# One product moved from VectorE to GpSimd, and the picks paired, in a top-k attention followed by a capacity-limited mixture of experts

## The chip, the core and the metric

The kernel runs on one NeuronCore of one Trainium2 chip. A core has five engines that run their own instruction queues in order and meet at semaphores: TensorE (PE: matrix products and transposes), VectorE (DVE), ScalarE (ACT), GpSimd (POOL), and SyncE (SP), which here only issues transfers. The metric is the device time of one execution in microseconds (us); lower is better. Before the change it is 997.43 us, the median of three runs (995.88 to 999.83).

## The reference

Attention over 8 batches of 8 heads, 576 tokens, head width 64, in which each row of scores keeps only its 32 largest entries; then a routing of the 4608 tokens to 8 experts, of which each takes the 80 tokens with the highest gate.

```python
def _attn_ref(q, k, v):                      # (8, 8, 576, 64)
    scores = scale * np.matmul(q, k.transpose(0, 1, 3, 2))
    kth = np.partition(scores, -32, axis=-1)[..., -32:-31]
    mask = scores >= kth
    scores = np.where(mask, scores, -1e9)
    attn = softmax(scores)                   # written out in the reference
    return np.matmul(attn, v)

def _moe_ref(x, w_gate, w1, w2, capacity):   # x (4608, 512), 8 experts, capacity 80
    logits = x @ w_gate
    expert_idx = np.argmax(logits, axis=1)
    gate_w = softmax(logits)[np.arange(N), expert_idx]
    for e in range(E):
        tok_idx = ...                        # the 80 tokens of expert e with the largest gate_w
        h = np.maximum(x[tok_idx] @ w1[e], 0.0)
        out[tok_idx] = gate_w[tok_idx, None] * (h @ w2[e])
```

## The kernel before

The attention part is a software pipeline. A *unit* is one tile of 128 query rows of one head, so a unit is a 128 x 576 tile of scores `s`; 32 pairs of heads have nine units each (four row tiles for each of two heads, and one last tile that holds the 64 remaining rows of both heads), 288 in all. They are numbered through, and a *step* `i` of the pipeline issues, for several units at once, the piece that each is due for. Steps come in pairs: an even one and an odd one.

For each unit the threshold is found so. Six maxima over sixths of the row give 48 candidates (`parts`); three rounds of "take the eight largest" over these give the 24th largest candidate (`search`). ScalarE then computes the sign of each score against that value and counts them; the scores times the signs are formed, the eight largest of that product are taken, and a *pick* by the count selects the threshold. `below` makes a mask of the scores that fall under it.

```python
def search(self, i):
    s, cand = self.s[i], self.top[i]
    ...
    for r in range(G0 // 8):                             # letters a, c, e: maxima
        dst = top[:, r, :] if r < G0 // 8 - 1 else w9[:, :8]
        nc.vector.max(out=dst, in_=cand)
        if r == G0 // 8 - 1:
            sign = self.rows.tile([P, S], BF16, name="sign", tag="sign")
            cnt = self.small.tile([P, 1], F32, name="cnt", tag="cnt")
            nc.scalar.activation(sign, s, Act.Sign, bias=w9[:, 7:8], scale=-1.0, accum_out=cnt)
        yield
        if r < G0 // 8 - 1:                              # letters b, d
            nc.vector.match_replace(out=cand, in_to_replace=dst, in_values=cand, imm_value=LOW)
            yield
    y = self.rows.tile([P, S], F32, name="y", tag="y", bufs=1)
    engine = nc.gpsimd if i in self.odd else nc.vector
    engine.tensor_tensor(out=y, in0=s, in1=sign, op=Alu.mult)   # letter y
    yield
    nc.vector.max(out=w9[:, 8:], in_=y)                  # letter g
    yield
    pick = ...
    nc.vector.scalar_tensor_tensor(out=pick, in0=past, scalar=cnt, in1=w9[:, 7:], accum_out=self.thr[:, i : i + 1],
                                   op0=Alu.is_equal, op1=Alu.mult)      # letter h
    yield

def below(self, i):                                      # letter m
    self.mask[i] = self.rows.tile([P, S], BF16, name="mask", tag="mask", bufs=3)
    if i in self.odd:
        nc.scalar.activation(self.mask[i], self.s[i], Act.Relu, bias=self.thr[:, i : i + 1], scale=-1.0)
        return
    nc.gpsimd.tensor_scalar(self.mask[i], self.s[i], self.thr[:, i : i + 1], None, op0=Alu.is_lt)
```

So before the change an even unit has its product on VectorE and its mask on GpSimd, an odd unit its product on GpSimd and its mask on ScalarE.

A step issues these pieces by a string of letters. `back` says how many steps after its own the unit gets the piece; `G` is one of the six maxima of the newest unit, and `z` a reciprocal of row sums.

```python
back = dict(a=0, b=1, c=1, d=1, e=1, y=2, g=3, h=4, m=4)
for c in "ghmGbGycGdGGGeaz" if i % 2 else "GbGhmgcGdGeGGyaz":
    ...
```

The remaining pieces of a step follow: `turn_w` (TensorE transposes the scores of a whole row tile and adds the masks, ScalarE takes the exponential), `front` (the scores of a later tile), `back` (the product with v, one step after `turn_w`), `divide`, and pieces of `norm`, which stores the result of a pair of heads and adds up its part of the gate's logits:

```python
def back(self, n, t):
    m = P if t < NF else TL                              # TL = 64 rows in the last tile
    for h in range(2):
        o = slice(2 * P + h * (D + 1), 2 * P + (h + 1) * (D + 1))
        j = h if t < NF else 0
        for c in range(NK):
            for r in range(0, m, TL):
                r0 = r if t < NF else TL * h
                nc.tensor.matmul(cc[r : r + TL, o], lhsT=wT[:, ..., r0 : r0 + TL], rhs=vb[:, c, h, :], ...)

# in norm
    nc.scalar.copy(part, lp[:, cs])
    yield 0
    if hp > 0:
        nc.vector.tensor_tensor(out=lg, in0=lg, in1=part, op=Alu.add)
```

Weights of experts 0 to 3 are loaded during the attention; expert 4 has a place of its own that comes free only when the attention's buffers do, and experts 5 to 7 follow into places that are done with. The part after the attention is routing (`route`) and eight experts (`finish`).

Of the kernel before, what the change touches and what calls it, by code (L numbers as in the profile page):

```python
# [9 lines left out]
F32 = mybir.dt.float32  # L10
# [4 lines left out]
Act = mybir.ActivationFunctionType  # L15
# [12 lines left out]
def kernel(  # L28
# [11 lines left out]
    nc = tc.nc  # L40
# [108 lines left out]
    class Attention:  # L149
# [95 lines left out]
        def search(self, i):  # L245

            s, cand = self.s[i], self.top[i]
            top = self.top[i] = self.small.tile([P, G0 // 8 - 1, 8], F32, name="top", tag="top")
            w9 = self.small.tile([P, 16], F32, name="w9", tag="w9")
            for r in range(G0 // 8):  # L250
# [8 lines that stand above are left out]
                if r < G0 // 8 - 1:  # L259
                    nc.vector.match_replace(out=cand, in_to_replace=dst, in_values=cand, imm_value=LOW)  # L260
                    yield
            y = self.rows.tile([P, S], F32, name="y", tag="y", bufs=1)
            engine = nc.gpsimd if i in self.odd else nc.vector
            engine.tensor_tensor(out=y, in0=s, in1=sign, op=Alu.mult)  # L264
            yield
            nc.vector.max(out=w9[:, 8:], in_=y)  # L266
            yield
            pick = self.small.tile([P, TOP_K - G0 + 1], F32, name="pick", tag="pick")
            nc.vector.scalar_tensor_tensor(out=pick, in0=past, scalar=cnt, in1=w9[:, 7:], accum_out=self.thr[:, i : i + 1],  # L269
                                           op0=Alu.is_equal, op1=Alu.mult)  # L270
            yield
# [10 lines left out]
        def search_all(self, i):  # L282

            s = self.s[i]
            top = self.top[i] = self.small.tile([P, TOP_K // 8, 8], F32, name="top", tag="top")
            scr = self.rows.tile([P, S], F32, name="y", tag="y", bufs=1)
            nc.vector.max(out=top[:, 0, :], in_=s)
            for r in range(1, TOP_K // 8):
                nc.vector.match_replace(out=scr, in_to_replace=top[:, r - 1, :], in_values=s if r == 1 else scr,
                                        imm_value=LOW)  # L290
                nc.vector.max(out=top[:, r, :], in_=scr)
            nc.vector.tensor_copy(self.thr[:, i : i + 1], top[:, TOP_K // 8 - 1, 7:8])
# [35 lines left out]
        def back(self, n, t):  # L328

            wT, cc = self.w.pop((n, t))  # L330
            vb = self.vb[n % len(self.vb)]
            m = P if t < NF else TL
            for h in range(2):
                o = slice(2 * P + h * (D + 1), 2 * P + (h + 1) * (D + 1))
                j = h if t < NF else 0
                for c in range(NK):
                    for r in range(0, m, TL):
                        r0 = r if t < NF else TL * h
                        nc.tensor.matmul(cc[r : r + TL, o], lhsT=wT[:, j * NF + c if c < NF else 2 * NF + j, r0 : r0 + TL],  # L339
                                         rhs=vb[:, c, h, :], start=(c == 0), stop=(c == NF))  # L340
            self.w[n, t] = cc

        def over(self, n, t):


            m = P if t < NF else TL
            sums = self.w[n, t][:m, 2 * P : 2 * P + 2 * (D + 1)].rearrange("p (h d) -> p h d", h=2)[:, :, D]
            z = self.z[:m, n % NP, t, :]
            if self.lean:
                nc.vector.tensor_scalar(z, sums, EPS, None, op0=Alu.add)  # L350
            nc.vector.reciprocal(z, z if self.lean else sums)  # L351

        def divide(self, n, t):
            m = P if t < NF else TL
            if t == 0:
                self.xn[n] = self.rows.tile([P, NK, 2, D], F32, name="xn", tag="xn")
            cc = self.w.pop((n, t))
            for h in range(2):
                o = 2 * P + h * (D + 1)
                nc.scalar.activation(self.xn[n][:m, t, h, :], cc[:m, o : o + D], Act.Copy, scale=self.z[:m, n % NP, t, h : h + 1])  # L360

        def norm(self, n, b, hp, bi, nb, cs=range(NK)):


            xn = self.xn[n].rearrange("p c h d -> p c (h d)")
            one, cols = bass.ds(b, 1), slice(hp * P, (hp + 1) * P)
            full = [c for c in cs if c < NF]
            if full:
                nc.sync.dma_start(xv[one, : NF * P, cols].rearrange("o (c p) d -> p (o c) d", p=P), xn[:, :NF, :])
            if NF in cs:  # L370
                nc.sync.dma_start(xv[one, NF * P :, cols].rearrange("o p d -> p o d"), xn[:TL, NF:, :])
            yield 1
            ps = self.four()[:, :2, :].rearrange("p j c -> p (j c)")
            at = slice(cs[0] * P, min(S, cs[-1] * P + P))
            self.turn_in(ps, xn, cs)
            xT = self.xT
            nc.scalar.copy(xT[:, at], ps[:, at])
            yield 1
            lp = self.four()[:, 0, : NK * E].rearrange("p (c e) -> p c e", e=E)
            for c in cs:  # L380
                for r in range(0, P, TL):
                    nc.tensor.matmul(lp[r : r + TL, c, :], lhsT=xT[:, c * P + r : c * P + r + TL], rhs=wg[:, hp, :],
                                     start=True, stop=True)
            if bi == 0 and hp == 0:
                self.lg = self.small.tile([P, nb, NK, E], F32, name="lg", tag="lg", bufs=2)
            cs = slice(cs[0], cs[-1] + 1)
            lg = self.lg[:, bi, cs]
            part = lg if hp == 0 else self.small.tile([P, NK, E], F32, name="part", tag="part", bufs=2)[:, cs]
            nc.scalar.copy(part, lp[:, cs])  # L389
            yield 0  # L390
            if hp > 0:
                nc.vector.tensor_tensor(out=lg, in0=lg, in1=part, op=Alu.add)
            if hp == HP - 1 and bi == nb - 1 and cs.stop == NK:
                yield 0
                yield from self.gates(b - bi, nb)
# [32 lines left out]
        def run(self, slow):  # L428
# [17 lines left out]
            def step(i, last):  # L446
# [7 lines left out]
                        due.append(n + 1)  # L454
                    first[i] = self.parts(i)

                back = dict(a=0, b=1, c=1, d=1, e=1, y=2, g=3, h=4, m=4)

                for c in "ghmGbGycGdGGGeaz" if i % 2 else "GbGhmgcGdGeGGyaz":
                    if c == "G":  # L460
                        if 0 <= i < NU:
                            next(first[i])
                    elif c == "a":
                        if 0 <= i < NU:
                            next(first[i], None)
                            second[i] = self.search(i)
                            next(second[i])
                    elif c == "z":
                        for u in drawn:
                            self.over(*u)  # L470
                    elif c == "m":
                        if 0 <= i - back[c] < NU:
                            self.below(i - back[c])
                    elif i - back[c] in second:
                        next(second[i - back[c]])
# [257 lines left out]
    def finish(wpool, full):  # L733

        stack = ctx.enter_context(ExitStack())
        late = stack.enter_context(tc.tile_pool(name="late", bufs=1))
        for dma in load_w(4, late):
            dma()
        sl = stack.enter_context(tc.tile_pool(name="sl", bufs=1))
        fs = stack.enter_context(tc.tile_pool(name="fs", bufs=2))  # L740
        ps_x = stack.enter_context(tc.tile_pool(name="ps_x", bufs=2, space=PSUM))
# [119 lines left out]

    slow = clear()
    with ExitStack() as main:
        wpool = main.enter_context(tc.tile_pool(name="wpool", bufs=4))
        for e in range(4):
            slow += load_w(e, wpool, 4)
        with ExitStack() as stack:
            att = Attention(stack, False)
            att.run(slow)
        finish(wpool, False)  # L870
    with tc.If(nc.values_load(bad[0:1, 0:1]) > 0):
# [4 lines left out]
            with tc.For_i(0, B) as b:  # L876
                att.batch(b)
        with ExitStack() as again:
            wpool = again.enter_context(tc.tile_pool(name="wpool2", bufs=4))
            for e in range(4):  # L880
                for dma in load_w(e, wpool):
                    dma()
            finish(wpool, True)
# [31 lines left out]
```

## Time and profile before

| | us |
|---|---|
| time, median of 3 runs | 997.43 |
| span of the profiled execution | 997.8 |
| of it up to the end of the attention's pipeline (last logits added) | about 870 |
| routing, to the first expert's gathered tokens | about 34 |
| eight experts and the stores | about 94 |

The share of busy time of an engine is an average over parts with different limits; the attention's pipeline is the longest part and the one that the change is about, so it is read by itself, in windows of 200 us. A line of a window gives start and end, length, then for each engine the time it was busy and the instructions in it, the clock that TensorE was granted, the share of the DMA engines and the rate. In groups of instructions, a line gives the source line, engine, operation, output and input with shapes and count, then the total and mean time, and last the idle time before such instructions with the one that ended it. In an excerpt of the timeline a line gives the start, the duration, and the instruction, and in brackets the idle time before it. On VectorE each instruction starts before the one ahead of it has fully drained, so what one adds to the queue is the distance from its start to the next start, and not its duration.

### The profile page before, as it was taken

To read this page: it belongs to the slowest core of one execution; us is meant where nothing else is said; L and a number is where in the kernel's file an instruction comes from. 1 tells how busy PE (TensorE), PEld (TensorE's weight loads), DVE (VectorE), ACT (ScalarE), POOL (GpSimd) and SP (SyncE) were. 2 spreads that over 40 slices of the span, in tenths; PEclk is the share of its full clock that TensorE was granted. 3 is DMA by queue.
4 is the path that set the end of the run, shared out by engine and by line. 5 is a ranking of instruction groups with operands and counts; after the bars stand their busy time and mean duration, and the time that the engine had idled before them with its cause. 6 is when DMAs were issued, how large, how long until landed. Compare 5 with 4: busy or idle time off the path is not lost.

```text
span 997.8 us, 35583 instructions
## 1 busy us (share of the span) xinstructions
PE 902.1 (90%) x13368; PEld 724.4 (73%) x13368; DVE 864.6 (87%) x5072; ACT 789.3 (79%) x1652; POOL 451.8 (45%) x330
## 2 busy tenths in 40 slices
PE   5899999999899999999899999998999998689996
PEld 3677777777777777777777777776777777578896
DVE  5999999999999999999999999999999999561110
ACT  3899999999889989999899999998899999501110
POOL 2455555545455455554454555554545455302111
PEclk9999999999999999999999999999999999978998
DMA  3445443333332323233332312222222200144920
GB/s 72 103 124 133 127 128 91 92 91 92 93 91 74 81 70 89 82 88 93 91 91 79 87 44 50 50 49 50 49 50 50 48 14 14 25 159 144 383 70 27
DMA packets 167893, 85.76 MB, mean 86 GB/s; under 512 B 117792, under 2 KB 154656, under 8 KB 167712
## 3 DMA queue, kind: packets, MB, share of 16 engines
q1 hardware_dynamic: 166688, 80.78, 29.3%
q0 software_dynamic: 1024, 2.62, 0.8%
q8 instruction: 107, 1.75, 0.7%
q14 instruction: 74, 0.61, 0.2%
HBM read 63.19 MB, written 20.19 MB: 84 GB/s over the span
## 4 chain that ended last, share of the span: by engine, by line
DVE 48%; PE 26%; ACT 19%; issue 6%; DMA 1%; POOL 0%; POOLq 0%; SPq 0%; ACTq 0%; DVEq 0%
DVE cand L241 15%; DVE w L266 11%; DVE cand L260 6%; DVE y L264 6%; PE cc L339 4%; PE sp L201 4%; ACT wT L325 4%; ACT sign L257 4%; PE yp L799 4%; ACT s L233 4%; DVE top L252 4%; ACT mask L278 3%; PE sp L226 3%; PE ab L316 3%; DVE pick L269 2%
## 5 line engine op out<-in xcount | busy, mean ns | idle before, releaser
L241 DVE MAX8 cand<-s 128x8 f32<-128x96 f32 x1728 | 388.6, 246 | 8.8 <-ACT s L233 8.8
L280 POOL TENSOR_SCALAR mask<-s,thr_all 128x576 bf16<-128x576 f32 x144 | 248.2, 1724 | 152.4 <-DVE pick L269 117.4
L264 POOL TENSOR_TENSOR y<-s,sign 128x576 f32<-128x576 f32 x144 | 184.7, 1283 | 271.9 <-DVE pick L269 125.7
L339 PEld LDWEIGHTS cc<-vb,wT 128*64 128x64 f32 x5760 | 199.3, 138 | 104.6 <-ACT wT L325 91.8
L339 PE MATMUL cc<-vb,wT 128*64 128x65 f32 x5760 | 221.6, 224 | 34.0 <-ACT wT L325 32.4
L257 ACT ACTIVATE sign<-s,w 128x576 bf16<-128x576 f32 x288 | 225.4, 783 | 24.3 <-DVE w L252 23.9
L266 DVE MAX8 w<-y 128x8 f32<-128x576 f32 x288 | 216.3, 751 | 2.5 <-POOL y L264 2.5
L226 PE MATMUL sp<-both 64*128 64x288 f32 (+1 forms) x1280 | 202.0, 435 | 15.0 <-ACT part L389 6.5
L233 ACT ACTIVATE s<-sp 128x1152 f32<-128x1152 f32 (+1 forms) x161 | 166.9, 1037 | 12.3 <-PE sp L226 12.3
L316 PE MATMUL ab<-ident,s 128*128 128x128 f32 x1148 | 174.9, 281 | 0.0
L325 ACT ACTIVATE wT<-ab 128x1024 f32<-128x1024 f32 (+1 forms) x159 | 148.9, 936 | 0.0
L226 PEld LDWEIGHTS sp<-both 64*128 64x128 f32 (+1 forms) x1280 | 105.5, 179 | 53.7 <-ACT part L389 8.5
L316 PEld LDWEIGHTS ab<-ident,s 128*128 128x128 f32 x1148 | 127.1, 141 | 11.6 <-issue 0.9
L321 PEld LDWEIGHTS <-mask 128*128 128x128 bf16 x1440 | 92.8, 98 | 34.8 <-POOL mask L280 18.9
L252 DVE MAX8 top<-cand 128x8 f32<-128x48 f32 x576 | 114.8, 199 | 0.0
L278 ACT ACTIVATE mask<-s,thr_all 128x576 bf16<-128x576 f32 x144 | 112.5, 781 | 0.0
L260 DVE MATCH_REPLACE8 cand<-top,cand 128x48 f32<-128x48 f32 x576 | 110.5, 192 | 0.1
L264 DVE TENSOR_TENSOR y<-s,sign 128x576 f32<-128x576 f32 x144 | 106.7, 741 | 1.3 <-ACT sign L257 0.8
L360 ACT ACTIVATE xn<-cc,z_all 128x64 f32<-128x64 f32 (+1 forms) x320 | 83.0, 318 | 1.3 <-DVE z_all L351 1.3
L316 PE MATMUL cc<-ident,s 128*128 128x128 f32 x288 | 78.7, 273 | 0.0
L323 ACT ACTIVATE wT<-cc 128x256 f32<-128x256 f32 (+1 forms) x160 | 56.6, 354 | 21.5 <-PE cc L321 20.8
L269 DVE SCALAR_TENSOR_TENSOR pick<-past,cnt,w 128x9 f32<-128x9 f32 x288 | 62.4, 217 | 0.0
(188 smaller groups left out, 964.0 us busy)
## 6 DMA issues: line engine op xcount, KB each, us to landing
w<-in_moe_w_dram SPq DMA_DIRECT2D x32, 512.0 KB, 4.3
w<-in_moe_w_dram SPq DMA_DIRECT2D x8, 2048.0 KB, 12.4
out_dram<-zero SPq DMA_DIRECT2D x9, 1024.0 KB, 6.5
qn<-in_q_dram SPq DMA_DIRECT2D x64, 128.0 KB, 2.5
kn<-in_k_dram SPq DMA_DIRECT2D x64, 128.0 KB, 2.4
vb<-in_v_dram SPq DMA_DIRECT2D x64, 128.0 KB, 2.4
xd<-xn SPq DMA_DIRECT2D x32, 256.0 KB, 4.1
qn<-in_q_dram SPq DMA_DIRECT2D x32, 32.0 KB, 2.3
```

The source lines that it names most:

```text
L226: nc.tensor.matmul(o, lhsT=qT[d, t * P : t * P + m], rhs=kT[d, j * HS : (j + 1) * HS], start=True, stop=True)
L233: nc.scalar.activation(s[:, j * HS : (j + w) * HS].rearrange("p (j c) -> p j c", c=HS), ps[:, j : j + w, :HS], Act.Copy, scale=TINY)
L241: nc.vector.max(out=cand[:, j, :], in_=s[:, j * S // NG : (j + 1) * S // NG])
L252: nc.vector.max(out=dst, in_=cand)
L257: nc.scalar.activation(sign, s, Act.Sign, bias=w9[:, 7:8], scale=-1.0, accum_out=cnt)
L260: nc.vector.match_replace(out=cand, in_to_replace=dst, in_values=cand, imm_value=LOW)
L264: engine.tensor_tensor(out=y, in0=s, in1=sign, op=Alu.mult)
L266: nc.vector.max(out=w9[:, 8:], in_=y)
L280: nc.gpsimd.tensor_scalar(self.mask[i], self.s[i], self.thr[:, i : i + 1], None, op0=Alu.is_lt)
L316: nc.tensor.matmul(dst[h][c], lhsT=sc[:, keys[c]], rhs=ident, start=c == 0 or (c == NF and h == 0), stop=False, is_transpose=True, skip_gr ...
L325: nc.scalar.activation(wT[:, : g * NF, :], ab.rearrange("p h c r -> p (h c) r")[:, : g * NF, :], Act.Exp, scale=scale / TINY)
L339: nc.tensor.matmul(cc[r : r + TL, o], lhsT=wT[:, j * NF + c if c < NF else 2 * NF + j, r0 : r0 + TL], rhs=vb[:, c, h, :], start=(c == 0), ...
```

## The change

All products by the sign now run on GpSimd, which takes VectorE's 144 of them away; `y` gets two buffers instead of one. The string of letters is rearranged: an odd unit's pick (`H`) and mask (`M`) come one step earlier in its life than before, right after the max over its product, so that both picks of a pair of steps stand side by side in the even step. In the even step the letters `m` (for the even unit whose pick is `h`) and then `y` (for the even unit two younger) both go to GpSimd, in that order; the max `g` over that `y` is the second letter of the odd step. For the last tile of a pair of heads the two heads' products with v go to the two halves of the output's partitions (and of the array's columns) rather than one after the other to the same half, so the reciprocal and the division read it there. The logits are added one step later. To pay for the buffers, the weights of expert 3 are no longer loaded during the attention but after it, ahead of those of expert 4.

```diff
-            y = self.rows.tile([P, S], F32, name="y", tag="y", bufs=1)
-            engine = nc.gpsimd if i in self.odd else nc.vector
-            engine.tensor_tensor(out=y, in0=s, in1=sign, op=Alu.mult)
+            y = self.rows.tile([P, S], F32, name="y", tag="y")
+            nc.gpsimd.tensor_tensor(out=y, in0=s, in1=sign, op=Alu.mult)
...
-            m = P if t < NF else TL
-            for h in range(2):
+            for h in range(2 if t < NF else 1):
                 o = slice(2 * P + h * (D + 1), 2 * P + (h + 1) * (D + 1))
-                j = h if t < NF else 0
                 for c in range(NK):
-                    for r in range(0, m, TL):
-                        r0 = r if t < NF else TL * h
-                        nc.tensor.matmul(cc[r : r + TL, o], lhsT=wT[:, j * NF + c if c < NF else 2 * NF + j, r0 : r0 + TL],
-                                         rhs=vb[:, c, h, :], start=(c == 0), stop=(c == NF))
+                    for r in range(0, P, TL):
+                        nc.tensor.matmul(cc[r : r + TL, o], lhsT=wT[:, h * NF + c if c < NF else 2 * NF + h, r : r + TL],
+                                         rhs=vb[:, c, h if t < NF else r // TL, :], start=(c == 0), stop=(c == NF))
...
             nc.scalar.copy(part, lp[:, cs])
             yield 0
+            yield 0
             if hp > 0:
                 nc.vector.tensor_tensor(out=lg, in0=lg, in1=part, op=Alu.add)
...
-                back = dict(a=0, b=1, c=1, d=1, e=1, y=2, g=3, h=4, m=4)
-
-                for c in "ghmGbGycGdGGGeaz" if i % 2 else "GbGhmgcGdGeGGyaz":
+
+                back = dict(a=0, b=1, c=1, d=1, e=1, y=2, g=3, h=4, m=4, H=3, M=3)
+                for c in "GgybGcGdGeGGza" if i % 2 else "GGghHmMybGcGdGeGza":
...
-        late = stack.enter_context(tc.tile_pool(name="late", bufs=1))
-        for dma in load_w(4, late):
-            dma()
+        late = stack.enter_context(tc.tile_pool(name="late", bufs=2))
+        for e in (3, 4):
+            for dma in load_w(e, late):
+                dma()
...
-        wpool = main.enter_context(tc.tile_pool(name="wpool", bufs=4))
-        for e in range(4):
+        wpool = main.enter_context(tc.tile_pool(name="wpool", bufs=3))
+        for e in range(3):
             slow += load_w(e, wpool, 4)
```

Left out of the diff: the same pool sizes in the fallback path, which does not run on these inputs, and the matching indices in `over` and `divide`.

More of the change, by code (lines that the diff above doesn't have):

```diff
@@ L285, in search_all @@
             top = self.top[i] = self.small.tile([P, TOP_K // 8, 8], F32, name="top", tag="top")
-            scr = self.rows.tile([P, S], F32, name="y", tag="y", bufs=1)
+            scr = self.rows.tile([P, S], F32, name="y", tag="y")
             nc.vector.max(out=top[:, 0, :], in_=s)
@@ L331, in back @@
             vb = self.vb[n % len(self.vb)]
-            m = P if t < NF else TL
-            for h in range(2):
+            for h in range(2 if t < NF else 1):
                 o = slice(2 * P + h * (D + 1), 2 * P + (h + 1) * (D + 1))
-                j = h if t < NF else 0
                 for c in range(NK):
-                    for r in range(0, m, TL):
-                        r0 = r if t < NF else TL * h
-                        nc.tensor.matmul(cc[r : r + TL, o], lhsT=wT[:, j * NF + c if c < NF else 2 * NF + j, r0 : r0 + TL],
-                                         rhs=vb[:, c, h, :], start=(c == 0), stop=(c == NF))
+                    for r in range(0, P, TL):
+                        nc.tensor.matmul(cc[r : r + TL, o], lhsT=wT[:, h * NF + c if c < NF else 2 * NF + h, r : r + TL],
+                                         rhs=vb[:, c, h if t < NF else r // TL, :], start=(c == 0), stop=(c == NF))
             self.w[n, t] = cc
         def over(self, n, t):
-            m = P if t < NF else TL
-            sums = self.w[n, t][:m, 2 * P : 2 * P + 2 * (D + 1)].rearrange("p (h d) -> p h d", h=2)[:, :, D]
-            z = self.z[:m, n % NP, t, :]
+            g = 2 if t < NF else 1
+            sums = self.w[n, t][:, 2 * P : 2 * P + 2 * (D + 1)].rearrange("p (h d) -> p h d", h=2)[:, :g, D]
+            z = self.z[:, n % NP, t, :g]
             if self.lean:
@@ L353, in divide @@
         def divide(self, n, t):
-            m = P if t < NF else TL
             if t == 0:
@@ L358, in divide @@
             for h in range(2):
-                o = 2 * P + h * (D + 1)
-                nc.scalar.activation(self.xn[n][:m, t, h, :], cc[:m, o : o + D], Act.Copy, scale=self.z[:m, n % NP, t, h : h + 1])
+                if t < NF:
+                    p, o, j, m = slice(0, P), 2 * P + h * (D + 1), h, P
+                else:
+                    p, o, j, m = slice(TL * h, TL * h + TL), 2 * P, 0, TL
+                nc.scalar.activation(self.xn[n][:m, t, h, :], cc[p, o : o + D], Act.Copy, scale=self.z[p, n % NP, t, j : j + 1])
         def norm(self, n, b, hp, bi, nb, cs=range(NK)):
@@ L470, in step @@
                             self.over(*u)
-                    elif c == "m":
+                    elif c in "mM":
                         if 0 <= i - back[c] < NU:
@@ L878 @@
         with ExitStack() as again:
-            wpool = again.enter_context(tc.tile_pool(name="wpool2", bufs=4))
-            for e in range(4):
+            wpool = again.enter_context(tc.tile_pool(name="wpool2", bufs=3))
+            for e in range(3):
                 for dma in load_w(e, wpool):
```

## The prediction

> **What bounds the kernel now.** I read the totals first, then windows inside the attention, then the waits of VectorE, and last the groups, for the durations that the change moves. The totals name three engines that are nearly full, and the windows tell which one sets the pace in the steady part.
>
> ```profile
> PE 902.1 (90%) x13368; PEld 724.4 (73%) x13368; DVE 864.6 (87%) x5072; ACT 789.3 (79%) x1652; POOL 451.8 (45%) x330
> ```
> ```profile
> 400.00:600.00 200.00, 185.30 (x2615) 146.65 (x2612) 196.23 (x1177) 183.22 (x381) 102.21 (x68) 1.00 0.30 81
> ```
>
> In 200 us of the attention VectorE is busy for 196 (98%), TensorE for 185, ScalarE for 183, GpSimd for 102. VectorE is the bound; TensorE and ScalarE stand 6 to 7% behind it. GpSimd's 68 instructions there are 34 masks and 34 products, one of each per pair of steps, so a pair now takes 200 / 34 = 5.88 us, and 144 pairs take 847 us of the 997. VectorE's waits say that it loses almost nothing:
>
> ```profile
> DVE lg L392 <- ACT part L389: 14.9, 16, 2.0
> ...
> DVE w L266 <- POOL y L264: 2.5, 2, 1.3
> ```
>
> The logits cost 14.9 us in 16 waits; GpSimd's product kept VectorE waiting twice in the whole run. Nothing on GpSimd is on the path today: its product is issued in the odd step and its mask in the even one, each with idle time before it.
>
> ```profile
> L280 POOL TENSOR_SCALAR mask<-s,thr_all 128x576 bf16<-128x576 f32 x144 | 248.2, 1724 | 152.4 <-DVE pick L269 117.4
> L264 POOL TENSOR_TENSOR y<-s,sign 128x576 f32<-128x576 f32 x144 | 184.7, 1283 | 271.9 <-DVE pick L269 125.7
> ...
> L266 DVE MAX8 w<-y 128x8 f32<-128x576 f32 x288 | 216.3, 751 | 2.5 <-POOL y L264 2.5
> ...
> L264 DVE TENSOR_TENSOR y<-s,sign 128x576 f32<-128x576 f32 x144 | 106.7, 741 | 1.3 <-ACT sign L257 0.8
> ```
>
> A product is 0.74 us on VectorE and 1.28 on GpSimd; the mask is 1.72.
>
> **What the Trainium skill says.** "Perfetto Trace Analysis", section Tensor Engine Instruction, states that ScalarE, VectorE and GpSimd are strict first-in-first-out; an instruction that is ready cannot pass one that waits. Its section GPSIMD Engine Instruction warns not to trust a GpSimd duration and to use the spacing of starts. Where the two kinds follow each other here the spacing is 28.47 - 27.22 = 1.25 us against 1.27 reported, so the durations hold to 0.02. "SBUF — State Buffer", section Who interferes with whom, states that a VectorE instruction with two SBUF inputs and a GpSimd instruction that reads SBUF block each other. The trace agrees: a pick (two such inputs) usually takes 0.21, and one that began inside a GpSimd product took 1.07 and ended with it.
>
> ```profile
> 34.37 1.29 POOL L264 TENSOR_TENSOR y<-s,sign 128x576 f32<-128x576 f32 x1 [4.17 <-DVE cand L241]
> ```
> ```profile
> 34.61 1.07 DVE L269 SCALAR_TENSOR_TENSOR pick<-past,cnt,w 128x9 f32<-128x9 f32 x1
> ```
>
> **Part 1, what VectorE gains.** One product per pair leaves its queue. Its start is 405.13 and the next start 405.79, so that is 0.66 us, 144 x 0.66 = 95 us in all. The logits' wait, 14.9 us, may go too with the later step. Both are an upper limit: TensorE needs 185.3 / 34 = 5.45 us per pair.
>
> **Part 2, what GpSimd takes on, and in what order.** Its work per pair becomes 1.72 + 2 x 1.28 = 4.28 us, 73% of today's pair. By throughput it fits. By order it does not. I read the order of the changed program: GpSimd's queue repeats mask, even product, odd product. The mask waits for the even unit's pick; the even product stands behind it, though its signs were ready long before; and the second letter of the odd step on VectorE is the max over that product. Between that pick and that max VectorE has only the second pick, two replacements, five maxima over sixths and three small ones: 2 x 0.13 + 2 x 0.17 + 5 x 0.16 + 3 x 0.11 = about 1.75 us. So I work out the loop, starting at the even unit's pick:
>
> ```profile
> 403.29 0.21 DVE L269 SCALAR_TENSOR_TENSOR pick<-past,cnt,w 128x9 f32<-128x9 f32 x1
> ...
> 403.42 0.75 DVE L266 MAX8 w<-y 128x8 f32<-128x576 f32 x1
> 404.10 0.19 DVE L252 MAX8 top<-cand 128x8 f32<-128x48 f32 x1
> ...
> 405.13 0.74 DVE L264 TENSOR_TENSOR y<-s,sign 128x576 f32<-128x576 f32 x1
> 405.79 0.20 DVE L252 MAX8 top<-cand 128x8 f32<-128x48 f32 x1
> ```
> ```profile
> 403.67 1.72 POOL L280 TENSOR_SCALAR mask<-s,thr_all 128x576 bf16<-128x576 f32 x1 [0.55 <-DVE pick L269]
> ```
> ```profile
> 27.22 1.27 POOL L264 TENSOR_TENSOR y<-s,sign 128x576 f32<-128x576 f32 x1 [4.34 <-DVE pick L269]
> 28.47 1.72 POOL L280 TENSOR_SCALAR mask<-s,thr_all 128x576 bf16<-128x576 f32 x1
> ```
> ```profile
> 28.53 0.76 DVE L266 MAX8 w<-y 128x8 f32<-128x576 f32 x1 [1.33 <-POOL y L264]
> ```
>
> - Start of the pick to start of the mask: 403.67 - 403.29 = 0.38. (The program's mask waits for the first of the two picks alone.)
> - Start of the mask to start of the product behind it: 1.72 - 0.02 = 1.70.
> - Start of the product to start of the max that waits for it: 28.53 - 27.22 = 1.31.
> - From there VectorE's own queue to the next even unit's pick, by distances of starts: the max over y twice, 2 x 0.67 = 1.34; seven maxima over sixths at 0.16 = 1.12; two replacements at 0.17 = 0.34; three small maxima at 0.11 = 0.33; together 3.13.
>
> The sum is 6.52 us. To this I add 0.04 for a reciprocal (0.07, on this stretch in half of the pairs) and 0.06 as my allowance for logits and gates: 6.62. Against 5.88 that is 0.74 more per pair, 144 x 0.74 = 107 us. VectorE would wait about 1.6 us in each odd step (0.38 + 1.70 + 1.31 = 3.39 less 1.75), where its max is said to wait for GpSimd's product.
>
> The odd product runs behind the even one and ends 0.38 + 1.70 + 1.26 + 1.28 = 4.62 after the pick; its max is due at 6.62 - 0.67 = 5.95, so it costs nothing, and GpSimd is idle again when the next two picks come, so they should not be blocked by the shared port. TensorE (5.45) and ScalarE (183.2 / 34 = 5.39) fit into 6.62.
>
> **Part 3, the last tile's products.** 10 products of 64 columns per pair of heads run in two halves of the array instead of one behind the other. In the chain after the attention 20 of the paired kind take 1.39 / 2 = about 0.7 us (40 take 1.39), so ten unpaired ones should take about as long and the pairing saves about 0.35 us in each of 32: 11 us of TensorE, off the path in either case. I count 0.
>
> **Part 4, the weights.** 4 MB move to the end of the attention, at about 870 us; in the window of 930 to 940 us the transfers ran at 390 GB/s, so about 11 us, beside routing. Expert 3 is computed from about 931 on by the chain of work, 60 us later. I count 0.
>
> **Sum.** 997.4 + 107 = 1104.
>
> **The rivals.** (a) *VectorE's relief is real and GpSimd keeps up*: then TensorE is next, 5.45 us per pair plus some gaps, say 5.55, and the time is 997 - 144 x 0.33 = 950. For it speak 98% on VectorE and 51% on GpSimd; against it the order of the queue, which a share cannot show. (b) *The port*: the added GpSimd time blocks picks and the logits' additions. If one pick per pair lost 0.9 us, as the one at 34.61 did, on top of part 2, the time would be 1104 + 130 = 1230. Against it: by my loop GpSimd has ended its last product about 2 us ahead of the picks. (c) *Weights late*: if expert 3 had to wait, 10 to 20 us more; the 60 us above speak against it. (d) *Half a loop*: GpSimd's mask could begin earlier than I count, or odd and even steps could shift so that only part of the 1.6 us shows; this would give 1040 to 1080.
>
> **Range and chances.** The loop is a chain of in-order queues with measured links, so I hold to 1104. An error of 0.1 us in a link is 14 us. Below it I allow for (d), above it for blocking of some additions and for ScalarE's signs coming late: 1080 to 1140. Only rival (a) makes it faster, and it needs the program order to be read wrongly: 0.03; within 2%: 0.02; slower: 0.95.
>
> **What would show it.** Right: VectorE busy about 87% in a window of the attention, with a wait of 1.4 to 1.8 us at the max over y in 144 places (200 to 250 us in total) laid to GpSimd's product; on GpSimd mask, product, product back to back, then about 2 us idle; a pair of about 6.6 us; picks of 0.21 us. Wrong: VectorE without such waits and TensorE near 97% (rival a); picks of a microsecond (rival b); waits for weights at expert 3 (rival c).

## The result and the profile after

The changed kernel takes 1121.36 us (1120.65 to 1122.05); the ratio to the kernel before is 1.124, 95% interval 1.1215 to 1.1262. It is 124 us slower.

First the totals, then the window in the middle of the attention:

```profile
PE 909.0 (81%) x13368; PEld 729.4 (65%) x13368; DVE 808.3 (72%) x4928; ACT 811.9 (73%) x1652; POOL 627.1 (56%) x474
```
```profile
400.00:600.00 200.00, 165.35 (x2299) 131.15 (x2299) 160.73 (x1003) 165.44 (x337) 126.75 (x90) 0.96 0.24 61
```

Before, VectorE was busy for 196 of these 200 us. Now no engine is near that: TensorE stands at 165, VectorE at 161, ScalarE at 165 and GpSimd at 127. No engine is full and yet the time is longer, so I looked for engines that wait for each other in a circle. GpSimd did 90 instructions, three to a pair of steps, so a pair takes 200 / 30 = 6.67 us instead of 5.88. VectorE's waits name the place:

```profile
DVE w L265 <- POOL y L263: 188.5, 143, 1.9
...
DVE lg L391 <- ACT part L387: 3.2, 2, 2.2
```

143 waits, in all but one of the 144 pairs, of 1.32 us on average, at the max over GpSimd's product; before there were two such waits. The wait for the logits has gone from 14.9 to 3.2 us. One turn of the circle, GpSimd first and then VectorE (start, duration, instruction, idle time before it):

```profile
487.32 1.72 POOL L279 TENSOR_SCALAR mask<-s,thr_all 128x576 bf16<-128x576 f32 x1 [2.46 <-DVE pick L268]
489.00 2.51 POOL L263 TENSOR_TENSOR y<-s,sign 128x576 f32<-128x576 f32 x2
493.98 1.72 POOL L279 TENSOR_SCALAR mask<-s,thr_all 128x576 bf16<-128x576 f32 x1 [2.46 <-DVE pick L268]
```
```profile
486.93 0.21 DVE L268 SCALAR_TENSOR_TENSOR pick<-past,cnt,w 128x9 f32<-128x9 f32 x1
...
490.31 0.76 DVE L265 MAX8 w<-y 128x8 f32<-128x576 f32 x1 [1.33 <-POOL y L263]
...
492.04 0.41 DVE L241 MAX8 cand<-s 128x8 f32<-128x96 f32 x2
492.48 0.21 DVE L252 MAX8 top<-cand 128x8 f32<-128x48 f32 x1
...
493.59 0.22 DVE L268 SCALAR_TENSOR_TENSOR pick<-past,cnt,w 128x9 f32<-128x9 f32 x1
```

GpSimd is idle for 2.46 us until the pick, does the mask, then the two products back to back; VectorE is idle for 1.33 us until the first product. Each engine waits for the other once per pair: 486.93 to 493.59 is 6.66 us.

All of the loss lies in this part. From the first to the last mask on GpSimd it was 838.1 us before (21.1 to 859.2) and is 959.6 now (22.6 to 982.2): 121.5 us more, of 121.1 more in the span. From the last addition of logits to the end it was 127.1 us and is 124.3.

### The profile page after: what moved, and what is told of

Its sections match the earlier page's. It is cut to its first block, busy times and chain, and to the rows that moved or that the text cites. A ratio compares the mean times of both kernels' runs of the same rounds, so it can differ in the third digit from the quotient of the medians.

```text
span 1118.9 us, 35622 instructions
## 1 busy us (share of the span) xinstructions
PE 909.0 (81%) x13368; PEld 729.4 (65%) x13368; DVE 808.3 (72%) x4928; ACT 811.9 (73%) x1652; POOL 627.1 (56%) x474
## 5 line engine op out<-in xcount | busy, mean ns | idle before, releaser
L241 DVE MAX8 cand<-s 128x8 f32<-128x96 f32 x1728 | 403.0, 248 | 9.3 <-ACT s L233 9.3
L263 POOL TENSOR_TENSOR y<-s,sign 128x576 f32<-128x576 f32 x288 | 365.2, 1279 | 42.3 <-ACT sign L257 42.0
L265 DVE MAX8 w<-y 128x8 f32<-128x576 f32 x288 | 216.7, 752 | 188.6 <-POOL y L263 188.5
L335 PEld LDWEIGHTS cc<-vb,wT 128*64 128x64 f32 x5760 | 194.7, 146 | 166.7 <-ACT wT L324 150.9
L335 PE MATMUL cc<-vb,wT 128*64 128x65 f32 x5760 | 217.7, 233 | 94.2 <-ACT wT L324 94.0
L226 PE MATMUL sp<-both 64*128 64x288 f32 (+1 forms) x1280 | 207.3, 444 | 17.5 <-ACT part L387 9.5
L315 PE MATMUL ab<-ident,s 128*128 128x128 f32 x1148 | 179.7, 286 | 0.0
L315 PEld LDWEIGHTS ab<-ident,s 128*128 128x128 f32 x1148 | 130.5, 144 | 11.9 <-issue 0.9
L320 PE MATMUL cc<-minus,mask 128*128 128x128 bf16 x144 | 32.3, 225 | 68.6 <-POOL mask L279 67.9
L358 ACT ACTIVATE xn<-cc,z_all 128x64 f32<-128x64 f32 (+1 forms) x320 | 85.4, 312 | 1.2 <-DVE z_all L347 0.8
```

What stands on the lines that cost most here:

```text
L226: nc.tensor.matmul(o, lhsT=qT[d, t * P : t * P + m], rhs=kT[d, j * HS : (j + 1) * HS], start=True, stop=True)
L241: nc.vector.max(out=cand[:, j, :], in_=s[:, j * S // NG : (j + 1) * S // NG])
L263: nc.gpsimd.tensor_tensor(out=y, in0=s, in1=sign, op=Alu.mult)
L315: nc.tensor.matmul(dst[h][c], lhsT=sc[:, keys[c]], rhs=ident, start=c == 0 or (c == NF and h == 0), stop=False, is_transpose=True, skip_gr ...
L320: nc.tensor.matmul(dst[h][c], lhsT=mk[:, keys[c]], rhs=huge if i + h in self.odd else minus, start=False, stop=True, skip_group_check=True)
L335: nc.tensor.matmul(cc[r : r + TL, o], lhsT=wT[:, h * NF + c if c < NF else 2 * NF + h, r : r + TL], rhs=vb[:, c, h if t < NF else r // TL, ...
```

## The experiments

The theory: the product is slow because of its place in GpSimd's queue, behind a mask that waits for VectorE, and ahead of a max that VectorE soon needs. The rivals: GpSimd's added work, or the port (rival b of the prediction: that work on GpSimd blocks VectorE); the new order of the letters; or one of the side parts. "us per pair" is the time from the first to the last mask on GpSimd, by 143. Ratios are to the kernel before, with their 95% interval.

| run | us | ratio | us per pair |
|---|---|---|---|
| before | 997.4 | | 5.86 |
| after | 1121.4 | 1.124 (1.1215 to 1.1262) | 6.71 |
| even product twice | 1312.0 | 1.312 (1.310 to 1.314) | 8.04 |
| odd product twice | 1142.8 | 1.143 (1.141 to 1.145) | 6.83 |
| max later | 993.8 | 0.995 (0.993 to 0.997) | 5.83 |
| product ahead of the mask | 1077.1 | 1.079 (1.076 to 1.082) | 6.34 |
| even product back on VectorE | 1063.1 | 1.064 (1.062 to 1.067) | 6.30 |
| old letters, all products moved | 1160.5 | 1.162 (1.158 to 1.165) | 6.97 |
| other parts alone | 1032.7 | 1.034 (1.032 to 1.036) | 6.09 |
| the same, one buffer for y | 997.6 | 0.998 (0.997 to 0.999) | 5.85 |
| max later, mask later | 986.5 | 0.987 (0.985 to 0.988) | 5.76 |
| and transposes split | 965.2 | 0.966 (0.964 to 0.968) | 5.61 |
| before, transposes split | 988.3 | 0.991 (0.988 to 0.993) | 5.80 |

### Order or amount: one product computed twice

The extra products write the same tile again, so the output stays as it was; GpSimd does 144 more of them in both runs.

```diff
             y = self.rows.tile([P, S], F32, name="y", tag="y")
-            nc.gpsimd.tensor_tensor(out=y, in0=s, in1=sign, op=Alu.mult)
+            for _ in range(1 if i in self.odd else 2):   # the other run: 2 if i in self.odd else 1
+                nc.gpsimd.tensor_tensor(out=y, in0=s, in1=sign, op=Alu.mult)
```

> The changed kernel with the even unit's product computed twice on GpSimd, one after the other into the same tile. My theory: the second one lies in the loop pick, mask, product, max: 1.26 us more in each pair, 144 x 1.26 = 181 us: 1290 to 1310 us. The rival, that what counts is GpSimd's work or its share of the port: the same for this run and the one with the odd product twice.

> The changed kernel with the odd unit's product computed twice on GpSimd. My theory: it ends 1.26 us later, at 4.62 + 1.26 = 5.9 us after the pick, and its max is due at about 6.0, so it costs little although GpSimd does 181 us more work: 1120 to 1145 us. The rival, GpSimd's work or its share of the port: as with the even product twice, 1290 us or more.

VectorE's waits in the two, the even product twice and then the odd one twice:

```profile
DVE w L266 <- POOL y L264: 380.2, 144, 3.3
```
```profile
DVE w L266 <- POOL y L264: 202.4, 178, 2.2
```

GpSimd is busy for 809 us in the one and 810 in the other, yet the first costs 191 us over the changed kernel and the second 21. Most pairs of the second still take 6.67 us. The first is 2 us above my range: three products in a row take 3.88 us where two took 2.51, so the added one is 1.37 us of the loop and not 1.26. So the same work is dear in one place of the queue and nearly free in another: the amount is not the cause, nor is the port by the time that GpSimd holds it. The order is.

### Moving the reader, with GpSimd's queue untouched

```diff
-                for c in "GgybGcGdGeGGza" if i % 2 else "GGghHmMybGcGdGeGza":
+                for c in "GybGcGdGeGGgza" if i % 2 else "GGghHmMybGcGdGeGza":
```

> The changed kernel with the max over the even unit's product moved from the second letter of the odd step to nearly its end (GybGcGdGeGGgza instead of GgybGcGdGeGGza); GpSimd's queue stays mask, product, product. My theory: the product ends about 3.4 us after the pick and the max is now due about 3.3 to 3.9 us after it, so the wait shrinks to under 0.2 us; GpSimd's loop is then 0.38 + 1.70 + 1.25 + 1.31 + 0.67 = 5.31 us, under TensorE's 5.45; 945 to 970 us. The rival, load or port: 1060 us or more. A third possibility, that only part of the stall goes since the odd product's max becomes due too early: 980 to 1020 us.

993.8 us: one letter takes back all of the loss (128 us), so the early max is the cause as far as the change's loss goes. But the gain is smaller than I expected: 993.8 lies in the third range, not in 945 to 970. GpSimd's timeline shows why:

```profile
403.19 1.72 POOL L279 TENSOR_SCALAR mask<-s,thr_all 128x576 bf16<-128x576 f32 x1 [1.10 <-DVE pick L268]
404.89 2.53 POOL L263 TENSOR_TENSOR y<-s,sign 128x576 f32<-128x576 f32 x2
408.52 1.73 POOL L279 TENSOR_SCALAR mask<-s,thr_all 128x576 bf16<-128x576 f32 x1 [1.10 <-DVE pick L268]
...
437.45 1.29 POOL L263 TENSOR_TENSOR y<-s,sign 128x576 f32<-128x576 f32 x1
439.91 1.27 POOL L263 TENSOR_TENSOR y<-s,sign 128x576 f32<-128x576 f32 x1 [1.17 <-ACT sign L257]
```

About half of the pairs (75 of 143) run at 408.52 - 403.19 = 5.33 us, GpSimd's own loop, worked out beforehand as 5.31. In others the odd product waits for its signs from ScalarE (74.9 us in all), and its max, early in the next even step, then waits for it (almost all of the 56.0 us of such waits in this run). The wait at the even product's max is gone, and another part of the chain is now the slowest.

### The product ahead of the mask

```diff
-                for c in "GgybGcGdGeGGza" if i % 2 else "GGghHmMybGcGdGeGza":
+                for c in "GgybGcGdGeGGza" if i % 2 else "GGyghHmMbGcGdGeGza":
```

> The changed kernel with the even unit's product issued ahead of the mask in GpSimd's queue (letters GGyghHmM instead of GGghHmMy), all else equal. My theory, the order of the queue: the product no longer stands behind a mask that waits for the pick, so VectorE's wait at the max over y goes and the pair is set by TensorE (5.45 us) with gaps; 945 to 985 us, the upper part if a product now runs into the picks and blocks them (picks of up to 0.7 us instead of 0.21). The rival, that GpSimd's greater load or the shared port costs the time: the load is the same, so 1060 us or more.

Missed: 1077 us, 44 better than the changed kernel and 92 above my range. VectorE's waits at the max fell from 188.5 to 76.3 us, and picks now run into products (0.39 us on average). But there is also a circle that I had not drawn. GpSimd, TensorE (a first product with the even mask) and ScalarE in one turn:

```profile
407.39 1.28 POOL L263 TENSOR_TENSOR y<-s,sign 128x576 f32<-128x576 f32 x1 [2.61 <-DVE cand L241]
408.65 1.73 POOL L279 TENSOR_SCALAR mask<-s,thr_all 128x576 bf16<-128x576 f32 x1
...
414.26 1.29 POOL L263 TENSOR_TENSOR y<-s,sign 128x576 f32<-128x576 f32 x1 [2.64 <-DVE top L252]
```
```profile
410.43 0.23 PE L320 MATMUL cc<-minus,mask 128*128 128x128 bf16 x1 [2.71 <-POOL mask L279]
```
```profile
406.45 0.78 ACT L257 ACTIVATE sign<-s,w 128x576 bf16<-128x576 f32 x1
...
410.69 0.39 ACT L322 ACTIVATE wT<-cc 128x256 f32<-128x256 f32 x1 [1.94 <-PE cc L320]
...
413.28 0.80 ACT L257 ACTIVATE sign<-s,w 128x576 bf16<-128x576 f32 x1
```

The product waits for its signs (which end at about 407.3), and the mask, whose pick was done at 406.5, stands behind it. In half of the pairs of heads TensorE needs the mask in that same step; ScalarE's exponentials wait for TensorE, and the signs for the next even product stand behind the exponentials. 407.39 to the next at 414.26 is 6.87 us. ScalarE's exponentials waited for TensorE at the mask 43 times here, 48.9 us in all, and 3 times in the changed kernel. How the rest of the loss divides between this circle and the picks that run into products stays open. Of the two orders tried in GpSimd's queue each makes one reader wait: the max over the product in the one, TensorE in the other.

### The even product back on VectorE, with the new letters

```diff
-            nc.gpsimd.tensor_tensor(out=y, in0=s, in1=sign, op=Alu.mult)
+            (nc.gpsimd if i in self.odd else nc.vector).tensor_tensor(out=y, in0=s, in1=sign, op=Alu.mult)
```

> The changed kernel with the even units' product back on VectorE, the new letters and all else kept. My theory: no GpSimd product stands behind a mask and in front of a max at once, so there is no wait at the max; VectorE is the bound again with 5.77 us per pair plus about 0.2 us of small gaps that the new letters leave: 985 to 1020 us. A rival, that the new letters (two picks side by side) cost the time and not the product's place: 1060 us or more.

Missed again: 1063 us, in the rival's range. There is hardly a wait at the max, as expected (6.6 us), but something else costs time. The letter `y` now stands right behind the pick that releases GpSimd's mask, so VectorE's product and the mask begin together, and which is first differs. VectorE and GpSimd, in a pair of each kind:

```profile
409.35 1.12 DVE L263 TENSOR_TENSOR y<-s,sign 128x576 f32<-128x576 f32 x1 [0.20 <-ACT sign L257]
...
435.24 0.75 DVE L263 TENSOR_TENSOR y<-s,sign 128x576 f32<-128x576 f32 x1
```
```profile
409.12 1.72 POOL L279 TENSOR_SCALAR mask<-s,thr_all 128x576 bf16<-128x576 f32 x1 [1.81 <-DVE pick L268]
...
435.29 2.29 POOL L279 TENSOR_SCALAR mask<-s,thr_all 128x576 bf16<-128x576 f32 x1 [1.65 <-DVE pick L268]
```

Where the mask is first it takes its 1.72 us and the product 1.12 instead of 0.74 (such pairs take 6.54 us); where the product is first it takes 0.75 and the mask 2.29 (5.90 us). Over the run the mask is first in 60 pairs and the product in 83. That they hold each other up agrees with the Trainium skill, "SBUF — State Buffer", section Who interferes with whom: a VectorE instruction with two inputs in SBUF contends with a GpSimd instruction that reads SBUF. VectorE also waits for signs here (24.7 us). So the new letters do cost time in this form; the run does not clear the letters as I meant it to, and says only that they were not made for a product on VectorE.

### The old letters with all products moved

The changed kernel with the two old strings, `"ghmGbGycGdGGGeaz"` and `"GbGhmgcGdGeGGyaz"`.

> All products on GpSimd, but with the old order of the letters (picks in different steps, max over the even product as the first letter of the odd step); the other parts as in the changed kernel. GpSimd's queue is again mask, even product, odd product. My theory: the same loop as in the changed kernel, 3.39 us from the even pick to the max, 0.67 for it, then the odd pick runs into the odd product on GpSimd and is held to about 4.6, and 2.2 us of VectorE to the next even pick: 6.8 us per pair, 1125 to 1160 us, with picks of 0.35 us on average. So pairing the picks would be worth 0 to 35 us by itself. The rival, that the new letters and not the move cost the time: under 1060 us.

1160.5 us, half a microsecond above the range and slower than the changed kernel: the move costs the time without the new letters too. The run of the next part (1032.7 us) differs from this one only in having the even product on VectorE, so with the old letters the move by itself costs 128 us. The new letters together are worth 39 us, a little more than I had for the paired picks; how much of it is the pairing, and how much the other places, this does not tell. One of the picks in the odd step, and the product that it ran into:

```profile
410.23 1.28 DVE L268 SCALAR_TENSOR_TENSOR pick<-past,cnt,w 128x9 f32<-128x9 f32 x1
```
```profile
410.21 1.27 POOL L263 TENSOR_TENSOR y<-s,sign 128x576 f32<-128x576 f32 x1 [0.69 <-ACT sign L257]
```

Picks take 0.45 us on average here (I had 0.35), 0.22 in the changed kernel, and the waits at the max come to 148.8 us.

### The other parts, and a buffer that was a lock

The changed kernel with the old letters and the old places of the products; then the same with `bufs=1` for `y`.

> The other parts alone: the old letters and the old places of the products, with the last tile's products in column halves, the logits' addition a step later and expert 3's weights after the attention. My theory: the logits' wait of 14.9 us on VectorE goes, and the other two parts are off the path: 980 to 992 us. The rival, that the late weights or the halves cost something: 998 us or more.

Missed: 1032.7 us, 34 slower than the runs of before beside it, and in the rival's range. Nothing waits for longer at VectorE. The group that grew is the pick, here of this run and of the one that followed it:

```profile
L268 DVE SCALAR_TENSOR_TENSOR pick<-past,cnt,w 128x9 f32<-128x9 f32 x288 | 104.8, 364 | 0.2 <-DVE z_all L347 0.2
```
```profile
L268 DVE SCALAR_TENSOR_TENSOR pick<-past,cnt,w 128x9 f32<-128x9 f32 x288 | 69.5, 241 | 0.2 <-DVE z_all L347 0.2
```

> The run with the other parts alone, but y with one buffer as before. In that run nothing waited longer, yet VectorE's picks took 0.36 us on average instead of 0.22 (104.8 us against 62.4 in all), each ending with a GpSimd product. Theory: with one buffer GpSimd's odd product has to wait for VectorE's max over the even product, and so it began only after the pick; with two buffers it begins as soon as its signs are there and the pick runs into it. With one buffer again: picks of 0.22 us and 980 to 990 us. The rival, that the late weights, the column halves or the later addition cost the 34 us: 1020 to 1035 us with picks of 0.22 us or not.

997.6 us. The second buffer alone, in this order of letters, costs 35 us. With one buffer, GpSimd's odd product must wait until VectorE has read the even one, and the pick slips in just then; with two it starts as soon as its signs are there, and VectorE's pick is caught by it. The idle time ahead of GpSimd's products says it: with one buffer 130.7 us of it ended with a pick, with two all 204.1 us ended with the signs. A product and a caught pick with two buffers, which end together:

```profile
402.97 1.28 POOL L263 TENSOR_TENSOR y<-s,sign 128x576 f32<-128x576 f32 x1 [0.72 <-ACT sign L257]
```
```profile
403.49 0.78 DVE L268 SCALAR_TENSOR_TENSOR pick<-past,cnt,w 128x9 f32<-128x9 f32 x1
```

The picks' 35.3 us more (104.8 - 69.5) are as much as the two runs differ by. A wait that looked like waste kept two engines apart.

My 980 to 990 did not come. The logits' wait is gone (3.4 us left), but the pairs of 6.78 us that held it became 6.1, with others of 5.66 grown to 5.9 and 6.1, and picks took 7 us more. What takes the gain back there stays open. The sum of the other parts is -2 us; a gain of the later addition and a cost of the column halves or of the late weights, each of at most some 15 us, could cancel in it.

### A version that beats both

With the later max, the signs were late. So the odd unit's mask on ScalarE goes behind the sign:

```diff
-                for c in "GybGcGdGeGGgza" if i % 2 else "GGghHmMybGcGdGeGza":
+                for c in "GybGcGdGeGGgza" if i % 2 else "GGghHmybGcGdGeMGza":
```

> The run with the later max (GybGcGdGeGGgza), with the odd unit's mask on ScalarE issued after the sign of the even step instead of ahead of it (GGghHmybGcGdGeMGza instead of GGghHmMybGcGdGeGza). There two thirds of the pairs took 5.32 us, GpSimd's own loop, and the others 6 to 7, mostly where GpSimd's odd product waited for ScalarE's signs (74.9 us in all). Theory: the mask of 0.78 us stands ahead of the sign that is needed sooner; with the mask behind it, the signs come 0.7 us earlier, and more pairs run at 5.32: 965 to 985 us. The rival, that ScalarE is simply full there: 988 to 998 us.

986.5 us: better by 7, but 1.5 us above the range, between it and the rival's. (Before this step half of the pairs ran at 5.33 us, and not two thirds, as I wrote.) A third of the pairs stays slow. In one of them, ScalarE and then GpSimd:

```profile
381.02 1.12 ACT L214 COPY both<-sp 128x1152 f32<-128x1152 f32 x1 [0.99 <-PE sp L201]
382.05 0.77 ACT L257 ACTIVATE sign<-s,w 128x576 bf16<-128x576 f32 x1
```
```profile
382.98 1.28 POOL L263 TENSOR_TENSOR y<-s,sign 128x576 f32<-128x576 f32 x1 [1.08 <-ACT sign L257]
```

The signs stand behind a copy that itself waits 0.99 us for ten transposes (of q and k of the next pair of heads). I cut that lump in two, q in one step and k in another:

```diff
+        def turn_half(self, n, j):
+            ps = self.four()[:, :2, :].rearrange("p j c -> p (j c)")
+            if j == 0:
+                both = self.qkp.tile([P, 2, S], F32, name="both", tag="both")
+                self.turned[n] = both[:, 0, :], both[:, 1, :]
+            self.turn_in(ps, self.qk[n][j].rearrange("p c h d -> p c (h d)"))
+            nc.scalar.copy(self.turned[n][j], ps[:, :S])
...
-                        due.append(n + 1)
+                        due.extend([(n + 1, 1), (n + 1, 0)] if n else [(1, None)])
...
-                    self.turn(due.pop())
+                    m, j = due.pop()
+                    self.turn(m) if j is None else self.turn_half(m, j)
```

> The run with the later max and the later mask, and the transposes of the next pair of heads' q and k in two halves, each in a step of its own, instead of both in one step. There a third of the pairs still took 6.1 to 6.5 us; TensorE and ScalarE had the transposes and their copy, or the logits, on top of the usual work in them, and signs came late. If it is the lumps that cost, halving the largest one gives 970 to 982 us; if the two halves only displace the logits' pieces into other full steps: 984 to 995 us.

965.2 us, better than I expected of it: 3.4% under the kernel before and 156 us under the changed one. The window, in which VectorE, TensorE and ScalarE stand at 93 to 97% together:

```profile
400.00:600.00 200.00, 186.28 (x2748) 149.00 (x2745) 191.39 (x1205) 194.32 (x411) 151.45 (x108) 1.00 0.24 59
```

Is that the move of the product, or only the split? The split alone in the kernel before:

> The kernel before, with the transposes of q and k split over two steps as in the 965 us run, and nothing else. If VectorE's product on its queue is what bounds the kernel before, the split gives it little, since its pairs take VectorE's 5.67 us: 985 to 998 us. If the lumps on TensorE and ScalarE were worth about 20 us there too, and moving the product brought nothing: 970 to 980 us.

988.3 us. The split alone gives 0.9%; with all products on GpSimd, their readers far enough away, and the other parts of the change, it is 3.4%. So the change with its max and mask moved does pay, by about 23 us. That it is the product's move that pays fits VectorE's relief, but it is not shown alone: the column halves also free about 19 us of TensorE (worked out below), and both kernels keep TensorE at 93% in the window.

## Why the prediction was right

The time on record was 1104 (1080 to 1140); it came to 1121. The cause was as predicted; the growth was 124 us where I had 107, and the difference is in one term. By the steps:

- *The four links of the loop.* Pick to mask 0.39 (487.32 - 486.93; I had 0.38). Mask to product 1.68 (1.70). Product to max 1.31 (1.31). Max to the next pick 493.59 - 490.31 = 3.28, where I had 3.13. That last term was mis-sized. The small max (letter `a`) now stands right behind the sixth maximum whose result it needs; two such maxima should move the queue on by 0.32 us, but 492.04 to 492.48 is 0.44. In the old letters another instruction stood between. This is 0.12 of the 0.15.
- *The allowances.* I added 0.04 for a reciprocal, which costs nothing, since it fits into that same gap of 0.12 (a pair with one at the end of its odd step took 6.67 as well), and 0.06 for logits and gates. The mean pair is 6.71, 0.05 above the common 6.66: right in size. Sum: 6.71 - 5.86 = 0.85 per pair and 143 pairs, 121.5 us.
- *VectorE's wait.* Expected 1.4 to 1.8 us in 144 places, 200 to 250 us; measured 1.32 us in 143, 188.5 us. The same gap and the second pick's own wait for the max fill some of the time before it. The busy share that I named, 87% of a window, contradicted my own loop, in which VectorE works for 5.0 of 6.62 us, or 76%; it is 80%.
- *GpSimd's odd product costs nothing, and the picks are not blocked.* Right: no wait at the even step's max in the turn shown, and picks of 0.22 us. The run with the odd product twice confirms the slack: 21 us for 180 us of work.
- *The other parts, counted as 0.* Their sum is -2 us with one buffer. That hides two faults in my working. The first is the buffer: I counted 14.9 us of logits as a possible gain, and nothing for the second buffer. With the old letters that buffer costs 35 us; in the changed kernel the picks stand together where GpSimd is idle, and they take 0.22 us. The second is the last tile, which I sized at half: each product of the program is two matmuls in the trace, so its ten products are 20 matmuls. One behind the other they took 1.38 us, as long as the 40 of a whole tile, and in two halves of the array they take 0.80. That saves 0.58 us in each of 32 tiles, 19 us of TensorE and not 11. First before, then in the changed kernel:

```profile
865.98 1.38 PE L339 MATMUL cc<-vb,wT 128*64 128x65 f32 x20 [0.69 <-ACT wT L325]
```
```profile
872.26 0.80 PE L335 MATMUL cc<-vb,wT 128*64 128x65 f32 x20
```

- *The rivals.* TensorE as the next bound (a): not in this change, where TensorE is at 83% of the window. The port (b) is real, as four of the runs show, but not in the changed kernel, whose picks take 0.22 us. Weights (c): the end is not longer. Half a loop (d): all of it showed.

My loop was right for the kernel that I was given, and a poor guide to the nearest variants: for two of them I expected 945 to 985 us and they took 994 and 1077, since I had closed the circle through VectorE and GpSimd alone, and not through ScalarE's and TensorE's queues. I wrote that nothing on GpSimd was on the path, but TensorE already waited for its mask before:

```profile
PE cc L321 <- POOL mask L280: 12.1, 21, 1.2
```

## What to carry to other kernels

Before moving work to an engine that is half idle, write down its queue in order and ask of each instruction what the one ahead of it waits for; a share of 51% says nothing about that. If the moved instruction stands behind one that waits for the engine it was taken from, move its reader later, by as much as the two together take: here one letter was worth 128 us. Then look for the next instruction that waits: the gain ends there. A second buffer takes a wait away, and with it whatever order that wait was keeping.

## What the hardware showed that I had not expected

The block between VectorE and GpSimd is not always for the whole of the other's instruction. A pick caught by a product (two inputs) ended with it (1.28 us, above), but VectorE's product that began 0.23 us into a 1.72 us mask (one input) took 1.12 us and so ended 0.37 us ahead of the mask; it was held for only 0.38. And TensorE's granted clock was lower in the runs in which TensorE was busy for less of the time: in the window from 400 to 600 us it was 1.00 before with TensorE busy for 93%, 0.96 in the changed kernel with 83%, and 0.87 with the even product twice with 77%. The busy share alone does not give it, though: between 950 and 980 us of the changed kernel the clock was 1.00 at 68%.
